# ReLU²-attention and a gated feed-forward: three blocks of k on ScalarE's queue instead of four, with k's first block cast first

## The chip, the cores and the metric

The kernel runs on one core of one Trainium2 chip. The metric is the device time of one execution in microseconds, the median of several. Times within an execution are counted from the start of the profiled span.

## The reference

The inputs are `q`, `k`, `v` of shape (8 batches, 12 heads, 448 positions, 64 dimensions) and the weights of a feed-forward layer, all f32.

```python
scores = scale * np.matmul(q, k.transpose(0, 1, 3, 2))   # scale = 1/sqrt(64)
attn = np.maximum(scores, 0.0) ** 2 / S                  # S = 448
attn_out = np.matmul(attn, v)
...
x = attn_out.transpose(0, 2, 1, 3).reshape(B * S, H * D) # (3584, 768)
h = x @ w_in                                             # (3584, 2048)
g = np.maximum(h, 0.0) + alpha * np.minimum(h, 0.0)
out = g @ w_out                                          # (3584, 768)
```

## The kernel before

The work is cut into 24 groups of four heads (a batch has three groups). The 448 positions of a head are held as 64 rows of 7 blocks, so a group's q or k is a tile of 128 partitions (two times 64 rows), 2 head pairs, 7 blocks and 64 dimensions. For each group q and k must be transposed so that the dimension lies on the partitions. For the first groups TensorE does it: `turn_pe` transposes some blocks with an identity matrix into a PSUM bank and copies them into a tile `T`, on VectorE ("D") or ScalarE ("A"), as each call says. Later groups use a DMA transpose.

Scores come one k block at a time: `sc` issues eight matmuls (`score_mm`, line 175) of one k block in `T` against all seven q blocks in `T`, into a pair of PSUM banks; a ReLU on ScalarE (line 184) or VectorE (line 186) brings them to SBUF as `rl`; `square` (line 194) squares them; `attnv` multiplies by v; `f1` and `f2` are the two feed-forward products. PSUM has eight banks, given out in turn by `take_pair` and `take_bank` to the one that was taken longest ago. TensorE is the busiest engine.

The order on each engine is written out by hand: the code runs under a manual schedule, and every engine executes its instructions in the order in which the code emits them. An instruction waits at the head of its engine's queue until what it reads is there.

The change is in the start, group 0. Its q and k come by three transfers. SyncE's queue loads all of q as f32 into `qfirst`; ScalarE's queue loads the first four blocks of k as f32 into `kfirst` (line 129); GpSimd's queue loads the other three blocks of k, cast to bf16 in flight, directly into `raw` (line 133). The f32 blocks are cast to bf16 by `cast0` (line 296) on ScalarE or VectorE, and then `turn_pe` (transposes on line 153, copies on line 156) builds `T`. While the data are under way, 36 matmuls of the identity (line 137) keep TensorE active.

Before, ScalarE's queue at the start is: casts of q blocks 4-5 and 6, casts of k blocks 0-1 and 2-3, copies into `T` of q 4-5, q 6, k 1, k 3, k 2, then the ReLU of score block 0. VectorE's is: casts of q 0-1 and 2-3, copies of q 0-1, q 2-3, k 0, the ReLU of score block 1, the copy of k 4-6, the squares of blocks 0 and 1. TensorE's is: transposes of q 0-1, q 4-5, q 2-3, q 6, k 0, k 1, k 3, k 2, scores 0, scores 1, transposes of k 4-6, scores 2, scores 3, transposes of group 1's q, scores 4 and 5, transposes of group 1's k.

Of the kernel before, what the change touches and what calls it, by code (L numbers as in the profile page):

```python
# [10 lines left out]
F32 = mybir.dt.float32  # L11
# [5 lines left out]
NJ = 7  # L17
# [3 lines left out]
def kernel(  # L21
# [10 lines left out]
    nc = tc.nc  # L32
    B, H, S, D = q.shape
# [11 lines left out]
    singles = ctx.enter_context(tc.tile_pool(name="singles", bufs=1))  # L45
# [40 lines left out]
    def take_bank():  # L86
        i = min(range(8), key=lambda i: (taken[i], i))
        take(i, 1)
        return psum[:, i]


    raw, vraw = {}, {}

    def load_qk(n, names="qk"):
        b, g = divmod(n, NG)
        for name in names:
            src = q if name == "q" else k
            t = raw_pool.tile([128, 2, NJ, D], BF16, tag=name, name=f"{name}raw")
            flat = src[b].rearrange("(m two) (pp j) d -> (two pp) m (j d)", two=2, j=NJ)
            nc.gpsimd.dma_start(out=t.rearrange("p m j d -> p m (j d)"), in_=flat[:, 2 * g:2 * g + 2])  # L100
            raw[(n, name)] = t

    def load_v(n):
        b, g = divmod(n, NG)
        t = v_pool.tile([128, 2, NJ, D], BF16, tag="v", name="vraw")
        flat = v[b].rearrange("(m two) (pp j) d -> (two pp) m (j d)", two=2, j=NJ)
        nc.gpsimd.dma_start(out=t.rearrange("p m j d -> p m (j d)"), in_=flat[:, 2 * g:2 * g + 2])  # L107
        vraw[n] = t
# [4 lines left out]
    def load_w_in(i):  # L113
        lo, hi = 512 * i, 512 * i + 512
        for hf in range(2):
            for e in range(2):
                nc.gpsimd.dma_start(out=w_in_sb[64 * hf:64 * hf + 64, :, e, lo:hi],  # L117
                                    in_=w_in_v[hf, e, :, :, lo:hi])
# [2 lines left out]
        for lo in range(lo, hi, step):  # L121
            nc.gpsimd.dma_start(out=w_out_sb[h][:, lo:lo + step], in_=w_out_v[:, lo:lo + step, COLS[h][0]:COLS[h][1]])

    FIRST = 4
    first, flat0 = {}, {}
    for name, src, eng, hi in (("q", q, nc.sync, NJ), ("k", k, nc.scalar, FIRST)):
        first[name] = singles.tile([128, 2, hi * D], F32, name=f"{name}first")
        flat0[name] = src[0].rearrange("(m two) (pp j) d -> (two pp) m (j d)", two=2, j=NJ)[:, :2]
        eng.dma_start(out=first[name], in_=flat0[name][:, :, :hi * D])
        raw[(0, name)] = raw_pool.tile([128, 2, NJ, D], BF16, tag=name, name=f"{name}raw")  # L130
    nc.sync.dma_start(out=alpha_sb, in_=moe_alpha.rearrange("(kf p) -> p kf", p=128))
    make_identity(nc, ident)
    nc.gpsimd.dma_start(out=raw[(0, "k")][:, :, FIRST:].rearrange("p m j d -> p m (j d)"),
                        in_=flat0["k"][:, :, FIRST * D:])
    warm = psum[:, 7, :128]
    for _ in range(36):
        nc.tensor.matmul(warm, ident, ident, start=True, stop=True)
    load_qk(1)
    load_v(0)
# [6 lines left out]
    def turn_pe(n, parts=(("q", 0, NJ, "D"), ("k", 0, NJ, "D"))):  # L146
        if n not in T:
            T[n] = T_pool.tile([128, 2, NJ, 128], BF16, tag="T", name="T")
        for name, lo, hi, eng in parts:
            ps = take_bank().bitcast(BF16)  # L150
            for j in range(lo, hi):
                for s in range(2):
                    nc.tensor.transpose(ps[64 * s:64 * s + 64, 128 * j:128 * j + 128], raw[(n, name)][:, s, j], ident)  # L153
            dst = T[n][:, "qk".index(name), lo:hi].rearrange("p j c -> p (j c)")
            copy = nc.vector.tensor_copy if eng == "D" else nc.scalar.copy
            copy(dst, ps[:, 128 * lo:128 * hi])  # L156
# [62 lines left out]
    def sc(chunks):  # L219

        for n, j, eng in chunks:
            late.append((n, j, relu(score_mm(n, j), eng)))
# [70 lines left out]

    def cast0(name, lo, hi, eng):
        copy = nc.vector.tensor_copy if eng == "D" else nc.scalar.copy
        copy(raw[(0, name)][:, :, lo:hi].rearrange("p m j d -> p m (j d)"), first[name][:, :, D * lo:D * hi])  # L296

    load_w_in(0)
    load_v(2)
    cast0("q", 4, 6, "A")  # L300
    cast0("q", 0, 2, "D")
    cast0("q", 6, 7, "A")
    cast0("q", 2, 4, "D")
    cast0("k", 0, 2, "A")
    cast0("k", 2, 4, "A")
    turn_pe(0, (("q", 0, 2, "D"),))
    turn_pe(0, (("q", 4, 6, "A"),))
    turn_pe(0, (("q", 2, 4, "D"),))
    turn_pe(0, (("q", 6, 7, "A"),))
    turn_pe(0, (("k", 0, 1, "D"),))  # L310
    turn_pe(0, (("k", 1, 2, "A"),))
    turn_pe(0, (("k", 3, 4, "A"),))
    turn_pe(0, (("k", 2, 3, "A"),))
    sc([(0, 0, "A")])
    sc([(0, 1, "D")])
    turn_pe(0, (("k", 4, 7, "D"),))
    load_qk(3)
    load_w_in(1)
    load_w_in(2)
# [243 lines left out]
```

## Time and profile before

| | before |
|---|---|
| time, median of 3 | 385.66 us (385.64 to 386.36) |
| profiled span | 383.8 us |
| PE busy | 374.8 us, 98% |
| VectorE busy | 266.3 us, 69% |
| ScalarE busy | 208.5 us, 54% |
| granted TensorE clock | 1.00 |

A timeline line gives the start, the time from the start of the first to the end of the last of a run of equal instructions, the engine, the line, the operation, the tile written and the tile read, and how many; in brackets, how long the engine sat idle before it and what ended that. PE is TensorE, ACT ScalarE, DVE VectorE, POOL GpSimd; `T<-psum` is a copy into `T`, `rl<-psum` a ReLU, `at<-rl` a square. The chain of waits is followed back from the last instruction of the program: each step goes to whatever released it. A DMA line ends with the size and the time from issue to landing.

### The profile page before, as it was taken

What the parts mean: (1) busy time and instruction counts of PE and PEld (TensorE: products, weight loads), DVE (VectorE), ACT (ScalarE), POOL (GpSimd) and SP (SyncE); (2) the same over time, 40 slices, a digit from 0 to 9 for tenths busy, and PEclk for the clock granted to TensorE, in tenths of its full rate; (3) what the DMA queues carried; (4) which work ended last, traced back from release to release, by engine and by line L of the source; (5) the groups of instructions that cost most, each with busy time, mean ns of one, the idle gap of its engine ahead of it and who ended that gap; (6) DMA issues with size and microseconds to landing.
All of it is one profiled execution on the core that took longest, in us unless ns stands there. A gap on an engine that the chain in (4) does not pass through costs nothing.

```text
span 383.8 us, 7855 instructions
## 1 busy us (share of the span) xinstructions
PE 374.8 (98%) x3179; PEld 206.0 (54%) x3200; DVE 266.3 (69%) x422; ACT 208.5 (54%) x339; POOL 68.3 (18%) x104
## 2 busy tenths in 40 slices
PE   7799999999999999999999999999999999999996
PEld 5454565555544455555565455544556445645554
DVE  3997988767757988688656887779855788526300
ACT  6988687445643754555444556546544465434321
POOL 8566050506302202022200222020000000000000
PEclk9999999999999999999999999999999999999999
DMA  9999989999998658597292772946045300120023
GB/s 160 186 204 202 184 138 209 168 196 114 233 203 134 106 110 120 106 127 120 55 165 61 128 122 50 167 86 110 15 89 84 77 0 16 43 68 2 14 70 83
DMA packets 73284, 43.42 MB, mean 113 GB/s; under 512 B 40352, under 2 KB 69792, under 8 KB 73248
## 3 DMA queue, kind: packets, MB, share of 16 engines
q0 software_dynamic: 26864, 22.45, 40.2%
q1 hardware_dynamic: 45952, 20.07, 27.2%
q8 instruction: 25, 0.41, 0.4%
q10 hardware_dynamic: 432, 0.39, 0.3%
q14 instruction: 11, 0.09, 0.1%
HBM read 45.62 MB, written 11.01 MB: 148 GB/s over the span
## 4 chain that ended last, share of the span: by engine, by line
PE 94%; DVE 2%; DMA 1%; ACT 1%; issue 0%; ACTq 0%; DVEq 0%
PE psum L238 38%; PE psum L263 38%; PE psum L175 9%; PE psum L204 8%; DMA qfirst<-in_q_dram 1%; DVE at L194 1%; DVE T L156 1%; DVE rl L186 0%; PE psum L153 0%; ACT osb L265 0%; ACT kraw L296 0%; ACT qraw L296 0%; ACTq L271 0%; ACT T L156 0%; DVEq L186 0%
## 5 line engine op out<-in xcount | busy, mean ns | idle before, releaser
L263 PE MATMUL psum<-w_out,gT 128*128 128x256 bf16 (+3 forms) x891 | 149.8, 322 | 1.1
L238 PE MATMUL psum<-xT,w_in_sb 128*128 128x448 bf16 x768 | 149.8, 353 | 0.0
L263 PEld LDWEIGHTS <-gT 128*128 128x128 bf16 x912 | 86.8, 98 | 64.2 <-issue 8.2
L238 PEld LDWEIGHTS <-w_in_sb 128*128 128x128 bf16 x768 | 73.6, 98 | 72.8 <-issue 6.0
L247 DVE SCALAR_TENSOR_TENSOR gT<-neg,beta_sb,psum 128x448 bf16<-128x448 f32 x128 | 83.5, 677 | 33.7 <-ACT neg L246 33.5
L246 ACT ACTIVATE neg<-psum 128x448 f32<-128x448 f32 x128 | 69.3, 547 | 60.3 <-PE psum L238 58.5
L184 ACT ACTIVATE rl<-psum 128x896 bf16<-128x896 f32 x112 | 97.7, 929 | 1.0 <-PE psum L175 1.0
L194 DVE TENSOR_TENSOR at<-rl 128x896 bf16<-128x896 bf16 x162 | 90.6, 618 | 0.0
L186 DVE TENSOR_SCALAR rl<-psum 128x896 bf16<-128x896 f32 x56 | 60.8, 1086 | 39.9 <-PE psum L175 39.8
L265 ACT COPY osb<-psum 128x256 f32<-128x256 f32 (+3 forms) x57 | 27.0, 473 | 104.7 <-PE psum L263 98.9
L175 PE MATMUL psum<-T 64*64 64x448 bf16 x672 | 45.4, 356 | 2.1 <-ACT rl L184 1.0
L100 POOL DMA_DIRECT2D qraw<-in_q_dram x23 | 16.6, 722 | 133.6 <-DVE perm L161 130.3
L204 PE MATMUL psum<-at,vraw 64*64 64x448 bf16 x672 | 36.2, 350 | 0.0
L175 PEld LDWEIGHTS <-T 64*64 64x64 bf16 x672 | 16.9, 105 | 20.9 <-issue 13.6
L204 PEld LDWEIGHTS <-vraw 64*64 64x64 bf16 x672 | 21.0, 106 | 11.7 <-issue 1.5
L215 DVE TENSOR_SCALAR xT<-psum 128x448 bf16<-128x448 f32 x24 | 15.0, 624 | 14.6 <-PE psum L204 10.8
L100 POOL DMA_DIRECT2D kraw<-in_k_dram x23 | 16.7, 727 | 7.8 <-DVE rl L186 5.2
L107 POOL DMA_DIRECT2D vraw<-in_v_dram x24 | 17.5, 731 | 2.9 <-DMA qraw<-in_q_dram 1.1
L214 ACT ACTIVATE xT<-psum 128x448 bf16<-128x448 f32 x24 | 13.4, 560 | 2.3 <-PE psum L204 2.3
L161 DVE COPY perm<-kraw 128x896 bf16<-128x896 bf16 x19 | 11.6, 609 | 0.8 <-DMA kraw<-in_k_dram 0.8
L161 DVE COPY perm<-qraw 128x896 bf16<-128x896 bf16 x19 | 11.6, 612 | 0.0
L117 POOL DMA_DIRECT2D w_in_sb<-in_moe_w_in_dram x16 | 10.1, 634 | 6.6 <-DMA w_in_sb<-in_moe_w_in_dram 2.9
(25 smaller groups left out, 43.0 us busy)
## 6 DMA issues: line engine op xcount, KB each, us to landing
out_dram<-osb SPq DMA_DIRECT2D x54, 128.0 KB, 2.4
vraw<-in_v_dram POOLq DMA_DIRECT2D x24, 224.0 KB, 8.1
qraw<-in_q_dram POOLq DMA_DIRECT2D x23, 224.0 KB, 5.3
kraw<-in_k_dram POOLq DMA_DIRECT2D x23, 224.0 KB, 6.6
out_dram<-osb SPq DMA_DIRECT2D x56, 64.0 KB, 2.2
w_in_sb<-in_moe_w_in_dram POOLq DMA_DIRECT2D x16, 192.0 KB, 8.1
w_out<-in_moe_w_out_dram POOLq DMA_DIRECT2D x4, 512.0 KB, 8.8
w_out<-in_moe_w_out_dram POOLq DMA_DIRECT2D x4, 256.0 KB, 8.7
```

The lines of the kernel that those rows point to most:

```text
L100: nc.gpsimd.dma_start(out=t.rearrange("p m j d -> p m (j d)"), in_=flat[:, 2 * g:2 * g + 2])
L161: nc.vector.tensor_copy(p[:, i], raw.pop((n, name)).rearrange("p s j d -> p j s d"))
L175: nc.tensor.matmul(ps[64 * c:64 * c + 64, r, :S], t[64 * r:64 * r + 64, 1, j, 64 * c:64 * c + 64], t[64 * r:64 * r + 64, 0, :, 64 * c:64 * ...
L184: nc.scalar.activation(rl, ps[:, :, :S], ACTF.Relu)
L186: nc.vector.tensor_scalar(rl, ps[:, :, :S], 0.0, None, ALU.max)
L194: nc.vector.tensor_tensor(a, rl, rl, ALU.mult)
L204: nc.tensor.matmul(ps[64 * s:64 * s + 64, r, :S], vv[64 * r:64 * r + 64, s, j, :], a[64 * r:64 * r + 64, s], start=(j == 0), stop=(j == NJ ...
L238: nc.tensor.matmul(ps, w_in_sb[:, km // 2, km % 2, bass.ts(ff, 128)], xT[b][:, km // 2, km % 2, :], start=(km == 0), stop=(km == KM - 1))
L246: nc.scalar.activation(neg, ps, ACTF.Relu, scale=-1.0)
L247: nc.vector.scalar_tensor_tensor(gT[b // 2][:, ff, (b % 2) * S:(b % 2) * S + S], neg, beta_sb[:, ff:ff + 1], ps, ALU.mult, ALU.add)
L263: nc.tensor.matmul(ps, gT[sb][:, ff, bass.ts(c, 128)], w_out_sb[h][:, ff, lo:hi], start=(ff == 0), stop=(ff == KF - 1))
L265: nc.scalar.copy(o[:, lo:hi], ps)
```

## The change

Three things change, all in group 0. ScalarE's queue loads k's blocks 0 to 2 instead of 0 to 3, and GpSimd's queue the other four. ScalarE casts k's block 0 alone, ahead of its casts of q, and k's blocks 1-2 only after its copies of q into `T`. The copies of k's blocks into `T` are divided anew: block 1 goes to VectorE by itself, block 2 stays on ScalarE, and block 3 is transposed and copied with the tail 4-6, by VectorE. There are two warm-up matmuls fewer. It is meant to have less f32 data of k to wait for and to cast before the first scores, and to give ScalarE fewer copies.

In the changed kernel ScalarE's queue is: cast k 0, casts q 4-5 and q 6, copies q 4-5 and q 6, cast k 1-2, copy k 2, then the ReLU of block 0. VectorE's is: casts q 0-1 and 2-3, copies q 0-1, q 2-3, k 0, k 1, the ReLU of block 1, the copy of k 3-6, the squares. TensorE's is: transposes q 0-1, q 4-5, q 2-3, q 6, k 0, k 1, k 2, scores 0, scores 1, transposes k 3-6, scores 2, scores 3, and on as before.

```diff
-    FIRST = 4
+    FIRST = 3
...
-    for name, src, eng, hi in (("q", q, nc.sync, NJ), ("k", k, nc.scalar, FIRST)):
-        first[name] = singles.tile([128, 2, hi * D], F32, name=f"{name}first")
+    for name, lo, hi, eng in (("q", 0, NJ, nc.sync), ("k", 0, FIRST, nc.scalar)):
+        t = singles.tile([128, 2, (hi - lo) * D], F32, name=f"{name}first{lo}")
+        eng.dma_start(out=t, in_=flat0[name][:, :, lo * D:hi * D])
...
-    for _ in range(36):
+    for _ in range(34):
...
+    cast0("k", 0, 1, "A")
+    cast0("q", 0, 2, "D")
     cast0("q", 4, 6, "A")
-    cast0("q", 0, 2, "D")
+    cast0("q", 2, 4, "D")
     cast0("q", 6, 7, "A")
-    cast0("q", 2, 4, "D")
-    cast0("k", 0, 2, "A")
-    cast0("k", 2, 4, "A")
     turn_pe(0, (("q", 0, 2, "D"),))
     turn_pe(0, (("q", 4, 6, "A"),))
     turn_pe(0, (("q", 2, 4, "D"),))
     turn_pe(0, (("q", 6, 7, "A"),))
     turn_pe(0, (("k", 0, 1, "D"),))
-    turn_pe(0, (("k", 1, 2, "A"),))
-    turn_pe(0, (("k", 3, 4, "A"),))
+    cast0("k", 1, 3, "A")
+    turn_pe(0, (("k", 1, 2, "D"),))
     turn_pe(0, (("k", 2, 3, "A"),))
     sc([(0, 0, "A")])
     sc([(0, 1, "D")])
-    turn_pe(0, (("k", 4, 7, "D"),))
+    turn_pe(0, (("k", 3, 7, "D"),))
```

More of the change, by code (lines that the diff above doesn't have):

```diff
@@ L122, in load_w_out @@
             nc.gpsimd.dma_start(out=w_out_sb[h][:, lo:lo + step], in_=w_out_v[:, lo:lo + step, COLS[h][0]:COLS[h][1]])
-    FIRST = 4
+    FIRST = 3
     first, flat0 = {}, {}
-    for name, src, eng, hi in (("q", q, nc.sync, NJ), ("k", k, nc.scalar, FIRST)):
-        first[name] = singles.tile([128, 2, hi * D], F32, name=f"{name}first")
+    for name, src in (("q", q), ("k", k)):
         flat0[name] = src[0].rearrange("(m two) (pp j) d -> (two pp) m (j d)", two=2, j=NJ)[:, :2]
-        eng.dma_start(out=first[name], in_=flat0[name][:, :, :hi * D])
         raw[(0, name)] = raw_pool.tile([128, 2, NJ, D], BF16, tag=name, name=f"{name}raw")
+    for name, lo, hi, eng in (("q", 0, NJ, nc.sync), ("k", 0, FIRST, nc.scalar)):
+        t = singles.tile([128, 2, (hi - lo) * D], F32, name=f"{name}first{lo}")
+        eng.dma_start(out=t, in_=flat0[name][:, :, lo * D:hi * D])
+        for j in range(lo, hi):
+            first[(name, j)] = t[:, :, (j - lo) * D:]
     nc.sync.dma_start(out=alpha_sb, in_=moe_alpha.rearrange("(kf p) -> p kf", p=128))
@@ L295, in cast0 @@
         copy = nc.vector.tensor_copy if eng == "D" else nc.scalar.copy
-        copy(raw[(0, name)][:, :, lo:hi].rearrange("p m j d -> p m (j d)"), first[name][:, :, D * lo:D * hi])
+        copy(raw[(0, name)][:, :, lo:hi].rearrange("p m j d -> p m (j d)"), first[(name, lo)][:, :, :D * (hi - lo)])
     load_w_in(0)
     load_v(2)
+    cast0("k", 0, 1, "A")
+    cast0("q", 0, 2, "D")
     cast0("q", 4, 6, "A")
-    cast0("q", 0, 2, "D")
+    cast0("q", 2, 4, "D")
     cast0("q", 6, 7, "A")
-    cast0("q", 2, 4, "D")
-    cast0("k", 0, 2, "A")
-    cast0("k", 2, 4, "A")
     turn_pe(0, (("q", 0, 2, "D"),))
```

## The prediction

> **What bounds the kernel now.** I read the page's part 4 first, then the chain of waits in order of time over the first 20 us, then the timelines of ScalarE (ACT), VectorE (DVE) and TensorE (PE), and the DMA view of the first 7 us.
>
> ```profile
> PE 94%; DVE 2%; DMA 1%; ACT 1%; issue 0%; ACTq 0%; DVEq 0%
> ```
>
> The chain is TensorE for 94% of the span. The rest is the start:
>
> ```profile
> 0.74 4.21 DMA qfirst<-in_q_dram
> ...
> 4.97 0.60 ACT qraw L296 x2
> 5.57 0.61 ACT kraw L296 x2
> 6.18 0.44 ACT T L156 x2
> ...
> 6.67 0.60 PE psum L175 x8
> ...
> 7.37 1.09 DVE rl L186
> 8.46 0.26 DVE T L156
> 8.72 1.07 DVE at L194 x2
> 9.79 1.06 DVE T L156 x2
> ...
> 16.05 0.57 PE psum L175 x8
> 16.62 1.34 PE psum L204 x28
> ```
>
> (Columns: start, length, what, all in us.) q lands at 4.95, ScalarE casts and copies until the first scores at 6.67; from 7.37 to 16.05 VectorE carries the chain without a hole worth naming; from 16.05 on it is TensorE. So a delay of VectorE's queue before 16 us goes one for one into the end, and that is where the change works.
>
> ```profile
> 4.97 0.60 ACT L296 CAST qraw<-qfirst 128x256 bf16<-128x256 f32 x2 [2.41 <-DMA qfirst<-in_q_dram]
> 5.48 0.70 ACT L296 CAST kraw<-kfirst 128x256 bf16<-128x256 f32 x2
> 6.09 1.03 ACT L156 COPY T<-psum 128x256 bf16<-128x256 bf16 x5
> 7.10 8.21 ACT L184 ACTIVATE rl<-psum 128x896 bf16<-128x896 f32 x10
> ```
>
> ScalarE: no gap from 4.97 to 15.3. Ten ReLUs in 8.21 us, so one starts every 0.80.
>
> ```profile
> 8.07 0.38 PE L175 MATMUL psum<-T 64*64 64x448 bf16 x4 [0.22 <-ACT rl L184]
> ```
>
> These are the scores of block 3. They wait for a PSUM pair only, freed by ScalarE's first ReLU (7.10 + 0.92 = 8.02). Their operand was ready since 7.12.
>
> ```profile
> qfirst<-in_q_dram SPq DMA_DIRECT2D x1, 448.0 KB, 4.2
> kfirst<-in_k_dram ACTq DMA_DIRECT2D x1, 256.0 KB, 4.6
> ```
>
> Both are issued at 0.74: q lands at 4.95, k at 5.34. k is the later one, and it still costs nothing before, because ScalarE casts q until 5.57 anyway.
>
> [...] instructions appear in the order that the code emits. A waiting head therefore holds everything behind it; my forecast rests on this. [...] 256 KB of k, issued together with 448 KB of q, land 0.4 us after it. [...] The warm-up shows it: its matmuls start every 0.107 us until 4.43 and every 0.056 after 4.6.
>
> **The change part by part.**
>
> *Transfers.* k on ScalarE's queue goes from 256 to 192 KB. In the DMA view of 0 to 7 us the slices around 4 us move 370 to 430 GB/s; at 400 the 64 KB are worth 0.16 us. So k lands at about 5.34 - 0.16 = 5.2 (bounds: 5.1, if the 261 GB/s of the stretch 2 to 4 us counts, and 5.37 for no gain), and q, sharing with it, at about 4.84. The rest of k grows by as much; it landed at 1.43 + 5.3 = 6.7 and would now land about 6.9, while its transposes come at 7.9 below: hidden. Two warm-up matmuls fewer end at 4.8 instead of 5.05; TensorE then waits for q anyway: nothing.
>
> *Work moved.* ScalarE loses one cast in size (two of 128x256, 0.40 each, become one of 128x128, 0.29, and one of 128x256) and two T copies of 128x128: one goes to VectorE alone (k's block 1), one joins VectorE's copy of k's tail, 512 columns in place of 384 (0.35 for 384 and 0.62 for 896, so 0.42). By issue spacing (cast 0.31 and 0.20, copy 0.16) ScalarE saves 0.11 + 0.32 = 0.43 us. It would gain that if it were only busy and never waiting.
>
> *Waits added.* There are three, and I walk the queues with the durations of before (an instruction on ScalarE starts some 0.09 before its predecessor's end; from an engine's end to a dependant's start 0.04 to 0.05; a transpose 0.22; four score matmuls 0.38; a PE switch between scores and transposes 0.15 to 0.3, as at 6.90 to 7.17 and 7.31 to 7.46).
>
> First wait: ScalarE's first cast is now k's block 0, which needs the later transfer. It runs 5.22 to 5.51. Behind it q 4-5 ends at 5.82 (was 5.38) and q 6 at 6.02 (was 5.57). TensorE, in order, stands at q 4-5: transposes of q 4-5, q 2-3, q 6 and k 0 start at 5.88, 6.01, 6.12, 6.18. All T copies of q and k 0 are done by 6.78 (ScalarE's q 6 at 6.75, VectorE's k 0 at 6.78).
>
> Second wait: k's blocks 1-2 are cast on ScalarE behind its two copies of q, 6.64 to 7.04. Their transposes are emitted before the first scores, so TensorE holds scores 0, whose operands are ready at 6.8, until they are through: transposes at 7.09 and 7.17, scores 0 at 7.33 (was 6.67). ScalarE's copy of block 2 ends at 7.73 and its first ReLU starts at 7.76 (was 7.10, +0.66). VectorE's copy of block 1 runs 7.38 to 7.61, scores 1 go 7.66 to 8.04, and VectorE's ReLU of block 1 starts at 8.17 (was 7.37, +0.80; the 0.13 from scores to this ReLU are those of before).
>
> Third wait: block 3's T copy is now part of VectorE's tail copy, behind that ReLU (1.09 long, next start 1.01 later): 9.18 to 9.59. Scores 3 start at 9.65 instead of 8.07. Queued behind them on TensorE are group 1's q transposes (8.38 before, now 9.95), scores 4 and 5, and group 1's k transposes (9.40 before; spacing from scores 3 of 1.33 is kept, so 10.98). ScalarE's ReLU of block 2 starts at 8.72 and ends at 9.63; its ReLU of block 3 can start only at 10.08 (was 8.71, +1.37), an idle stretch of some 0.45. VectorE, after squares 0 and 1 and group 1's q copy, which ends near 11.2, waits for the last k transpose at 11.56 and copies at 11.60; before it did so at 10.24.
>
> *Sum.* VectorE's copy of group 1's k is late by 11.60 - 10.24 = 1.36; ScalarE's ReLUs are late by 1.37 to 1.40. From there on both queues hold the same work as before without slack (both busy 2.00 of every 2 us in the window sums from 10 to 18), so group 2's T copies, and TensorE's scores at 16.05, come 1.4 later, and so does the end: 385.66 + 1.4 = 387.06. The 0.43 us taken off ScalarE are spent inside its waits.
>
> **The rivals.**
>
> *k lands with or ahead of q* (the smaller transfer overtakes). Then wait one vanishes: q's casts start at about 4.86, scores 0 near 6.76, VectorE's ReLU near 7.6; but scores 3 still wait for the tail copy, to 9.09, and group 1's k copy comes at about 11.03: +0.8, 386.45. Against it: equal numbers of packets, and k last in the trace.
>
> *Faster.* If scores 0 were limited by ScalarE's amount of work, as the chain's 1.65 us of ScalarE pieces (4.97 to 6.62) suggest, taking off 0.43, and 0.11 for q's earlier landing, would give 385.12. Against it: transposes of k 1-2 stand ahead of the scores in the queue, and two of the three waits are not work of ScalarE.
>
> *Absorbed.* Some of the delay falls into holes: TensorE is busy only 1.3 to 1.6 of every 2 us between 9 and 17 us. About half lost, 386.2. Against it: VectorE and ScalarE, which set those holes, have none themselves.
>
> *Clock lost.* [...] The scores and transposes of about 2 us of TensorE work then take up to twice as long, half of it exposed: 1 us more, 388.1. Against it: the pauses are under 1 us each, and before had some of 0.6 without harm.
>
> **How the numbers follow.** The walk 58%, k early 14%, absorbed 10%, faster 10%, clock 8%. The likeliest gives 387.06. With k's landing between 5.1 and 5.37 the walk spans +1.26 to +1.55; k early and absorbed reach down to 386.2, and 0.2 to 0.3 for my switching times goes below that: 386.0. The high end, 387.7, has the same margin above the walk. Outside lie the faster and the clock case, under 2 in 10. 0.2% is 0.77 us. Over it lie the walk, the clock and half of k early (which sits on the line): 0.73. Within it lie the other half of k early, the absorbed case and half of the faster one: 0.22. The rest, 0.05, is a faster case that also closes some of TensorE's holes between 9 and 17 us.
>
> **What would show it.** Right: kfirst lands near 5.2, ScalarE's first cast starts at that landing and not at q's; the first scores start near 7.3, behind k 1-2's transposes; scores 3 wait for a VectorE T copy and start near 9.65; ScalarE has a hole ahead of its third ReLU; the scores at 16.05 move to about 17.4, and from there to the end nothing differs. Wrong: kfirst landing before 5.0, first scores before 6.7, or the delay at the 16 us scores not reaching the end.

## The result, and the profile after

| | before | after |
|---|---|---|
| time, median of 4 | 385.67 us (385.64 to 386.36) | 388.82 us (388.40 to 389.07) |
| profiled span | 383.8 us | 387.3 us |

The changed kernel is slower by 3.15 us, a ratio of 1.0076 (95% interval 1.0059 to 1.0094). The direction was forecast; the size, 1.4 us, was less than half of it.

The chain of waits of the changed kernel, in order of time (start, length, what, in us):

```profile
0.74 4.88 DMA kfirst<-in_k_dram
...
5.64 0.30 ACT kraw L299
...
7.35 0.31 ACT kraw L299
...
7.71 0.42 PE psum L156 x4
8.13 0.92 PE psum L178 x7
...
9.15 1.09 DVE rl L189
10.25 0.34 DVE T L159
...
19.74 0.57 PE psum L178 x8
```

The chain begins with k's transfer, no longer q's, and goes to and fro between ScalarE and TensorE: this is the queue that the prediction walked. But group 2's scores come at 19.74 instead of 16.05, 3.7 us late, not 1.4. From there to the end nothing is added; the span is 3.5 us longer.

ScalarE's timeline shows the holes in brackets:

```profile
5.64 0.30 ACT L299 CAST kraw<-kfirst 128x128 bf16<-128x128 f32 x1 [3.09 <-DMA kfirst<-in_k_dram]
...
8.70 0.92 ACT L187 ACTIVATE rl<-psum 128x896 bf16<-128x896 f32 x1 [0.27 <-PE psum L178]
10.16 0.92 ACT L187 ACTIVATE rl<-psum 128x896 bf16<-128x896 f32 x1 [0.54 <-PE psum L178]
11.27 0.92 ACT L187 ACTIVATE rl<-psum 128x896 bf16<-128x896 f32 x1 [0.19 <-PE psum L178]
```

Before, ScalarE had none between 4.97 and 15.3. And TensorE's timeline, in three stretches:

```profile
1.36 3.81 PE L140 MATMUL psum<-ident 128*128 128x128 bf16 x34 [1.36 <-POOL ident masks.py:199]
...
8.06 0.96 PE L178 MATMUL psum<-T 64*64 64x448 bf16 x8
...
10.63 0.59 PE L178 MATMUL psum<-T 64*64 64x448 bf16 x4 [0.52 <-DVE T L159]
...
18.51 0.57 PE L178 MATMUL psum<-T 64*64 64x448 bf16 x8
```

The eight score matmuls at 8.06 take 0.96 us; the same eight take 0.57 at 18.51, and took 0.57 before at 6.67. A single score matmul takes 0.58 us until 16.2 and 0.35 to 0.37 from 18.5. The 34 warm-ups start every 0.107 us to the last. So TensorE's clock was at half until 16.8, where the trace records its first change, and not only until 4.55, as in the kernel before. Nothing in the queues explains that.

This profile is of the slowest of the four executions. The other three carry a mean granted clock of 0.991: 0.009 of 386.6 us is 3.5 us, which is what 7 us at half clock lose. So by this estimate they lost the clock too, after a first release.

One theory was left, and three rivals. *Walk*: the three waits cost 1.4 us, or 1.8 with k landing at 5.62 instead of 5.2, and the half clock comes on top as an effect of its own. The rivals: the clock explains it all; the two warm-ups fewer are what lost the clock; or the moment of release is drawn anew at each execution, and the times scatter.

### The profile page after: what moved, and what is told of

Same layout as the page of the kernel before. It is cut to its first block, busy times and chain, and to the rows that moved or that the text cites. A ratio compares the mean times of both kernels' runs of the same rounds, so it can differ in the third digit from the quotient of the medians.

```text
span 387.3 us, 7872 instructions
## 1 busy us (share of the span) xinstructions
PE 379.1 (98%) x3198; PEld 207.4 (54%) x3198; DVE 266.5 (69%) x423; ACT 209.0 (54%) x337; POOL 68.2 (18%) x104
## 4 chain that ended last, share of the span: by engine, by line
PE 95%; DVE 2%; DMA 1%; ACT 1%; issue 0%; ACTq 0%; DVEq 0%
PE psum L241 38%; PE psum L266 38%; PE psum L178 9%; PE psum L207 8%; DMA kfirst<-in_k_dram 1%; PE psum L156 1%; DVE at L197 1%; DVE T L159 0%; DVE rl L189 0%; ACT osb L268 0%; ACT kraw L299 0%; ACT T L159 0%; ACTq L274 0%; ACT qraw L299 0%; DVEq L189 0%
## 5 line engine op out<-in xcount | busy, mean ns | idle before, releaser
L178 PE MATMUL psum<-T 64*64 64x448 bf16 x672 | 47.1, 371 | 1.4 <-DVE T L159 1.4
```

What stands on the lines that cost most here:

```text
L178: nc.tensor.matmul(ps[64 * c:64 * c + 64, r, :S], t[64 * r:64 * r + 64, 1, j, 64 * c:64 * c + 64], t[64 * r:64 * r + 64, 0, :, 64 * c:64 * ...
```

## The experiments

Each is timed against runs of the kernel before on the same chip, and "over before" is the difference of the two medians.

### Is it the number of warm-ups?

`a36` and `a40` are the changed kernel with 36 and 40 warm-ups, `b34` is the kernel before with 34.

```diff
-    for _ in range(34):
+    for _ in range(36):
```

> The changed kernel with 36 warm-up matmuls instead of 34, nothing else. In the changed kernel's trace TensorE's matmuls run at half clock until 17.0 us (warm-ups every 0.107 us to the last one, 128x448 score matmuls 0.58 us), in the kernel before only until 4.5 us. Theory count (the two warm-ups fewer keep the clock from being released): clock released near 4.5 us again, time 387.1 +- 0.3. Theory pauses (TensorE's longer waits after 4.9 us do it): as the changed kernel, 388.4 to 389.1. Theory phase ([...] the release time is drawn at each execution): the runs scatter between 387 and 389 whatever the count.

> The changed kernel with 40 warm-up matmuls, which reach to about 5.6 us at half clock and so up to the first transposes. Theory count: 387.1 +- 0.3, clock released by 5 us. Theory pauses: between 387.3 and 388.8, since the first pause (4.97 to 5.50) is filled and the two later ones are not. Theory phase: scatter between 387 and 389.

> The kernel before with 34 warm-up matmuls instead of 36, nothing else. Theory count: the clock is released late here too, and the time rises by 1 to 2.5 us, to 386.7 to 388.2. Theory pauses: 385.7, as before, since the warm-ups end before q lands in either case. Theory phase: scatter.

Measured: `a36` 388.46 (2.84 over before), `a40` 388.44 (2.82; one of four executions at 387.04), `b34` 385.57 (0.05 under before). The two warm-ups were not it: given back they recover about 0.3 us at most (the intervals of `a36`, 1.0054 to 1.0084, and of the changed kernel overlap), and taken from the kernel before they cost nothing. Nor do the times scatter freely: of the twelve executions of the changed kernel, `a36` and `a40`, eleven lie between 388.29 and 389.12.

The windows view suggests why. The trace of `a36` records the clock from 6.04 us on: full for 3.41 us, then half for 10.24, three times as long, then full. Here it is divided at these changes and every 3.41 us (stretch, its length, then the busy time of PE, PEld, DVE, ACT and POOL, granted clock, DMA share, GB/s; PEld is TensorE's loading of weights). In the first row the clock reads 1.00 only because the record has not begun; the warm-ups in it start every 0.107 us, at half clock:

```profile
2.63:6.04 3.41, 3.12 (x32) 2.69 (x30) 0.86 (x3) 0.67 (x3) 3.41 (x6) 1.00 1.23 210
6.04:9.46 3.42, 2.12 (x36) 1.08 (x36) 1.78 (x6) 2.69 (x7) 2.47 (x5) 1.00 1.22 186
9.46:12.87 3.41, 3.03 (x40) 1.76 (x40) 2.02 (x4) 2.29 (x4) 2.01 (x3) 0.50 1.26 203
12.87:16.28 3.41, 2.99 (x32) 1.17 (x27) 3.15 (x6) 3.35 (x5) 1.57 (x3) 0.50 1.18 168
16.28:19.70 3.42, 3.31 (x45) 2.24 (x48) 3.42 (x7) 3.03 (x5) 2.20 (x4) 0.50 1.23 196
19.70:23.11 3.41, 3.38 (x72) 2.38 (x65) 3.20 (x7) 3.41 (x6) 1.89 (x4) 1.00 1.25 204
```

Read the PE column against the clock of the next row. The warm-ups and first transposes fill 3.12 of 3.41 us, 91%, and the clock is full in the next window. In that one TensorE, kept waiting, is busy 2.12 us, 62%, and the clock falls to half. After 89% and 88% it stays at half; after 97% it is full, from 19.7 on. Here is the kernel before, divided the same way:

```profile
1.14:4.55 3.41, 3.19 (x31) 3.19 (x32) 0.00 (x0) 1.28 (x1) 3.28 (x6) 1.00 0.73 211
...
11.38:14.79 3.41, 2.32 (x44) 1.36 (x43) 3.41 (x7) 3.41 (x5) 1.54 (x3) 1.00 1.15 168
```

The window of the warm-ups has 94%, and the emptiest of the start after it 68%: in this profile the clock never falls there. The changed kernel's own profile begins with windows of 79%, 84% and 85% at half clock, and only after the fourth, 94%, is the clock full, from 16.78 on:

```profile
3.13:6.54 3.41, 2.70 (x30) 2.20 (x29) 0.79 (x3) 0.80 (x3) 3.41 (x6) 1.00 1.33 218
...
13.37:16.78 3.41, 3.21 (x34) 1.32 (x31) 2.86 (x6) 3.36 (x5) 1.97 (x3) 1.00 1.15 155
```

### Do fillers in the waits give the clock back?

`afill` puts 14 identity matmuls into TensorE's two longer early waits. `ahold` adds 40 warm-ups, 10 matmuls ahead of scores 3, and issues the score matmuls of five blocks twice (same bank, same result). `bhold` is the control, the kernel before with these five blocks doubled. In the excerpt below the first two additions are in both `afill` and `ahold`; the third is `ahold`'s alone, and the last is in `ahold` and `bhold`.

```diff
+    fill(6)
     turn_pe(0, (("q", 4, 6, "A"),))
...
     cast0("k", 1, 3, "A")
+    fill(8)
     turn_pe(0, (("k", 1, 2, "D"),))
...
+    fill(10, 6)
     sc([(0, 3, "A")])
...
+        for rep in range(2 if (n, j) in AGAIN else 1):
```

> The changed kernel with 34 warm-ups and 14 more matmuls of the identity in TensorE's two later waits: six ahead of the transposes of q's blocks 4-5, eight ahead of those of k's blocks 1-2. They write the bank of the warm-ups, which is free then. Theory count: as the changed kernel, 388.4 to 389.1, clock released late. Theory pauses: clock released by about 8 us instead of 17, time 387.1 to 387.9. Theory phase: scatter.

> The changed kernel with TensorE kept busy: 40 warm-ups, 6 and 8 identity matmuls in its two early waits, 10 ahead of scores 3, and the score matmuls of blocks (0,6) and (1,0) to (1,3) issued twice into the same bank with the same result. If the changed kernel's loss is the queue walk (1.4 us, with k landing at 5.4 instead of 5.2: 1.5) plus the half clock (the rest of 3.15), the clock now stays up from about 5 us on and the time is 387.1 +- 0.3. If the walk is wrong and the clock explains it all, 385.7 to 386.2. If filling cannot hold the clock, as with the 14 fillers, 387.6.

> The kernel before with the score matmuls of blocks (0,6) and (1,0) to (1,3) issued twice, as the control: what the doubled matmuls themselves cost. The kernel before falls in a part of its executions to 386.2 to 386.4 with a granted clock of 0.996. If that is a lost clock window in the sparse stretch from 11 to 15 us, these executions vanish and all lie at 385.5 to 385.7. If the doubled matmuls are on the path: slower, up to 386.4.

Measured: `afill` 387.61 (1.99 over before), `ahold` 387.38 (1.72; ratio 1.0044, interval 1.0029 to 1.0059), `bhold` 385.61 (0.05 under; 0.9996, 0.9987 to 1.0004). More work for TensorE took 1.43 us off the changed kernel's 3.15. In `afill`'s profile the clock still fell once, behind its sparse stretch:

```profile
11.84:15.25 3.41, 2.04 (x26) 0.76 (x25) 3.36 (x7) 3.41 (x6) 1.78 (x3) 1.00 1.21 176
15.25:18.66 3.41, 3.26 (x44) 2.26 (x44) 3.41 (x7) 3.01 (x6) 2.15 (x4) 0.50 1.20 187
```

60% busy at full clock, then half. That one window may have cost little: two of `afill`'s four executions carry a mean clock of 1.00 and are at most 0.12 us faster (though 1.00 can hide a late first release), and `afill` and `ahold` can't be told apart by their times (`afill`'s ratio is 1.0044 too). In `ahold`'s profile the clock is full from 4.64 us on. What remains is seen in its chain:

```profile
5.55 0.30 ACT kraw L301
...
17.78 0.57 PE psum L180 x8
```

Group 2's scores are 1.73 us late, with every matmul after the warm-ups at full speed. The doubled matmuls cost the kernel before nothing, and the executions at 386.2 to 386.5 that `b34` and the kernel before have are gone in `bhold` (12 executions, all at or below 385.89). They too look like a lost window: their mean clock is 0.996, which is about 3 us at half, and none of the 44 executions of `bhold`, `b_w1` and `b_w3`, all with the doubled blocks, carries it. No profile shows one.

### Does the clock alone cost time, without a changed queue?

`b20` is the kernel before with 20 warm-ups instead of 36 (the edit is the count).

> The kernel before with 20 warm-up matmuls instead of 36: no queue and no wait is changed, and the warm-ups end at 3.5 us, before q lands. If the clock follows the share of busy time in windows of 3.41 us (0.92 or more needed to release it, as the profiles so far show), it is released late or not before 10 us, and the time rises by 1 to 2.5 us with nothing else changed. If the clock loss comes only with the changed kernel's waits: 385.5 to 386.4 as before.

Measured: 386.44, 0.86 over before (1.0018, 1.0011 to 1.0025), a little under the low end expected. Its windows:

```profile
3.23:6.64 3.41, 1.78 (x27) 1.32 (x24) 1.24 (x5) 1.70 (x7) 3.41 (x6) 1.00 1.30 212
6.64:10.06 3.42, 3.42 (x42) 1.78 (x44) 2.27 (x5) 2.77 (x6) 2.42 (x4) 1.00 1.24 192
```

No release after 52%; matmuls at half speed then fill the next window entirely, and the clock is full from 10.06 on. So here a late release cost 0.86 us without any wait of the changed kernel. In the changed kernel's profile the half clock lasts longer, to 16.78, through windows of 79%, 84% and 85% to the one of 94%.

### What is each wait worth, with the clock held?

`ahold_no1` and `no1` cast k's block 0 behind ScalarE's casts of q (wait one out); `ahold_no2` casts k's blocks 1-2 ahead of ScalarE's copies (wait two out); `no12` does both. `no1` and `no12` have 36 warm-ups, the doubled blocks and no fillers ahead of q 4-5, and `no12` none ahead of k 1-2 either. The edit of `no12`'s queue, against the changed kernel:

```diff
-    cast0("k", 0, 1, "A")
     cast0("q", 0, 2, "D")
     cast0("q", 4, 6, "A")
     cast0("q", 2, 4, "D")
     cast0("q", 6, 7, "A")
+    cast0("k", 0, 1, "A")
+    cast0("k", 1, 3, "A")
...
-    cast0("k", 1, 3, "A")
     turn_pe(0, (("k", 1, 2, "D"),))
```

> The filled changed kernel with k's block 0 cast behind ScalarE's two casts of q instead of ahead of them (wait one of the walk taken out, the others kept). Walk: q's casts start at q's landing again, scores 0 come 0.5 earlier, and so the time falls by 0.4 to 0.6 against the filled changed kernel, to about 386.6. If wait one is hidden by the two behind it: no difference (within 0.15).

> The filled changed kernel with k's blocks 1-2 cast directly behind ScalarE's casts of q, ahead of its copies of q (wait two of the walk taken out, the others kept). Walk: scores 0 then wait for ScalarE's copy of q 6 only, about 0.4 to 0.5 earlier, so the time falls by 0.3 to 0.5 against the filled changed kernel. If the scores' start does not set the end: no difference (within 0.15).

> Wait one again, since in the last such run the 40 warm-ups and the six fillers behind them ran at half clock to 6.1 us and stood on the path themselves. Now 36 warm-ups, no fillers ahead of q's blocks 4-5, the other fillers kept; k's block 0 cast behind ScalarE's casts of q. Walk: scores 0 at 7.0 to 7.2 instead of 7.68, time 0.4 to 0.6 under the filled changed kernel's 387.2 to 387.4, so 386.8 +- 0.2. If wait one is hidden by the others: 387.2 to 387.5.

> Waits one and two out: ScalarE casts q 4-5, q 6, k 0 and k 1-2 and only then copies; 36 warm-ups, fillers only ahead of scores 3. What is left of the change is wait three (block 3 in VectorE's tail copy) and block 1's copy on VectorE. Walk: scores 0 near 6.8, scores 3 near 8.9 (before 8.07), time 386.1 to 386.4. If wait three costs nothing: 385.6 to 385.8.

`ahold_no1` (387.70) does not answer the question. In its profile the 40 warm-ups ran at half clock, and they and the six fillers behind them stood on the path: first scores at 8.27. `ahold_no2` (387.18, against 387.38 for `ahold`) gained 0.2, less than expected and less than its executions spread; there the eight fillers stand on the path in place of the wait. Without such fillers, `no1` is at 386.57 (1.08 over before) and `no12` at 385.89 (0.40 over), both a little faster than expected. So wait one is worth 1.72 - 1.08 = 0.64 us, wait two 1.08 - 0.40 = 0.68, and 0.40 are left for wait three, less what little `no12` gains ahead of it. The split is rough: `ahold` has four executions from 387.17 to 387.93, and in the slower ones its fillers may stand on the path as in `ahold_no1`. In the profiles group 2's scores are 1.73 us late in `ahold`, 0.96 in `no1` (17.01) and 0.41 in `no12` (16.46), which gives 0.77, 0.55 and 0.41. `no12`'s chain:

```profile
4.90 0.60 ACT qraw L301 x2
...
6.52 0.60 PE psum L180 x8
...
7.22 1.09 DVE rl L191
8.31 0.34 DVE T L159
...
8.70 0.38 PE psum L180 x4
```

It starts from q again, and the first scores come at 6.52, 0.15 before the 6.67 of the kernel before. Of that 0.07 is q's earlier landing; the rest, 0.08, is ScalarE's saved work. Then VectorE's ReLU and its tail copy stand ahead of scores 3, at 8.70 instead of 8.07.

### Waits three and one by themselves

`ahold_no3` and `no123` take wait three out by giving block 3 a transpose and a ScalarE copy of its own. `b_w3` goes the other way and puts it, alone, into the kernel before; `b_w1` puts wait one there (both with the doubled blocks of `bhold`). `no123` is `no12` with this edit and without the ten fillers ahead of scores 3, which `ahold_no3` leaves out too.

```diff
# ahold_no3, no123
-    turn_pe(0, (("k", 3, 7, "D"),))
+    turn_pe(0, (("k", 3, 4, "A"),))
+    turn_pe(0, (("k", 4, 7, "D"),))
# b_w3
-    turn_pe(0, (("k", 3, 4, "A"),))
...
-    turn_pe(0, (("k", 4, 7, "D"),))
+    turn_pe(0, (("k", 3, 7, "D"),))
# b_w1
+    cast0("k", 0, 2, "A")
     cast0("q", 4, 6, "A")
...
-    cast0("k", 0, 2, "A")
```

> The filled changed kernel with wait three alone out: block 3 transposed behind scores 1 and copied by ScalarE behind its first ReLU, VectorE's tail copy 384 columns again. Walk: scores 3 at about 9.4 instead of 10.0, time 0.4 to 0.6 under the filled changed kernel's 387.2 to 387.4, so 386.8 +- 0.2. If scores 3 are not what holds group 1's transposes: no difference.

> All three waits out: as the last one, and block 3 transposed by itself behind scores 1 and copied by ScalarE behind its first ReLU, so that scores 3 don't wait for VectorE; 36 warm-ups, no fillers but the doubled score matmuls, which cost the kernel before nothing. k still loads three blocks on ScalarE's queue. Walk: what remains is 0.1 to 0.3 us of ScalarE's order, time 385.6 to 386.0. If the smaller transfer of k itself costs something: above 386.2.

> Wait three alone, put into the kernel before (with the doubled score matmuls, which cost it nothing): block 3 of k is transposed and copied with blocks 4-6 by VectorE behind its first ReLU, and nothing else is changed. Walk, with the 0.43 us that the kernel with waits one and two taken out still lay behind: scores 3 at 8.8 to 8.9 instead of 8.07, time 386.0 to 386.3. If a score block that waits for VectorE instead of ScalarE costs nothing: 385.5 to 385.7.

> Wait one alone, put into the kernel before (with the doubled score matmuls): ScalarE casts k's blocks 0-1 ahead of its casts of q, so that q waits for k's landing. k still comes as four blocks. Walk: everything of ScalarE behind the first cast is late by k's landing minus q's (5.37 - 4.95) plus nothing, so 0.4 us, time 386.0 +- 0.2. If k's landing is not what holds ScalarE: 385.5 to 385.7.

`no123` (386.07, 0.58 over before) and `ahold_no3` (387.16, 1.67 over) missed their expectations: taking wait three out gave nothing. One more group of transposes takes one more PSUM bank, and the code gives out the bank that was taken longest ago. The tail's transposes then take a bank of the pair that scores 2 had. Scores 2 go onto the pair of scores 0, behind ScalarE's ReLU, and scores 3 onto the pair of scores 1, behind VectorE's. `ahold_no3`'s timeline of TensorE:

```profile
9.84 0.38 PE L180 MATMUL psum<-T 64*64 64x448 bf16 x4 [0.34 <-ACT rl L189]
10.44 0.38 PE L180 MATMUL psum<-T 64*64 64x448 bf16 x4 [0.21 <-DVE rl L191]
```

Scores 2 (the first line) now wait for a ReLU, which they did not before, and so do scores 3. A new wait took the old one's place. (In this profile, as in `ahold_no1`'s, warm-ups and fillers at half clock also stand on the path; in `no123`'s there are no fillers.)

`b_w3` shows wait three from the other side: 386.14, 0.56 over before (1.0007, 1.0000 to 1.0014, at the edge of what can be told), and its profile is plain. TensorE's timeline there:

```profile
8.88 0.38 PE L177 MATMUL psum<-T 64*64 64x448 bf16 x4 [0.95 <-DVE T L156]
```

Scores 3 wait 0.95 us for VectorE's copy and start at 8.88, as expected (8.8 to 8.9). `b_w1` is at 385.97, 0.39 over before (0.9999 to 1.0016 as a ratio, so at the edge too), the 0.4 that the two landings differ by; its ScalarE starts at 5.35 with k instead of 4.97 with q.

## Why the prediction was wrong

**Direction and path: right.** The chain moved as forecast. ScalarE's first cast waits for k, TensorE holds the first scores behind k 1-2's transposes, and scores 3 wait for VectorE's tail copy. The order within a queue held in the trace: q has landed by 5.16, when VectorE casts its part of it; ScalarE casts its own part only at 5.85, behind the cast of k that waited until 5.64. With the clock held (`ahold`), ScalarE's hole ahead of its third ReLU is 0.43 us, against 0.45 forecast.

**The walk's sum: right, but for one term.** At held clock the three waits measure 1.72 us (the interval is 1.1 to 2.3) against 1.4 forecast. Taken out one after another they are 0.64, 0.68 and 0.40, which add up to 1.72 by construction; put alone into the kernel before, wait one is 0.39 (k there lands 0.4 after q) and wait three 0.56, which is evidence of its own. Wait two was not put in alone. The term that was mis-sized is the landing of k. I took off 0.16 us for 64 KB less, to 5.2. In the ten profiles with three blocks k took 4.5 to 4.8 us from its issue, and 4.9 in the changed kernel's first; in the six with four blocks 4.6 to 4.7. The smaller transfer lands no sooner. In `ahold`'s profile (4.8, cast at 5.55 instead of 5.22) that is the missing 0.33: its first scores start at 7.68, against 7.33 in my walk, and group 2's scores are 1.73 late, against 1.4. With the usual landing, 4.6, the miss is about half of that. Why 64 KB don't matter was not tried; k's queue has 272 packets in either kernel, only shorter ones after the change.

**The step that failed: "Clock lost", 8%.** I set it aside because "the pauses are under 1 us each, and before had some of 0.6 without harm". That looks at each pause by itself. What the profiles show beside a lost clock is how much TensorE did in a whole 3.41 us window: `a36`, `afill` and `a40` (6.74 to 10.15, busy 1.90 of 3.41 us) lost it after 62%, 60% and 56%, and the kernel before, which kept it, had 68% in its emptiest. I had sized the effect at 1 us, from some 2 us of TensorE work at half speed (in `a36` the half clock lasted 10.24 us), and put it in the wrong place, as a rival instead of a term: the waits that I had just summed are TensorE's idle time, so the more of them I found, the emptier its windows became. With fillers to hold its clock the changed kernel loses 1.72 us instead of 3.15. The other 1.43 is the clock's part by subtraction; that the 1.72 is the waits' is borne out by the walk, which gives 1.73 once k's landing in `ahold`'s profile is put in.

**The claim that two warm-ups fewer cost nothing: right** in the kernel before (`b34`); in the changed kernel they cost 0.3 us at most (`a36`).

**The rivals "k early", "faster" and "absorbed": wrong.** No profile shows k ahead of q; ScalarE's saved work is real but small (0.08 us at the first scores of `no12`) and spent by wait three; and of the delay at group 2's scores no more than about 0.2 us is absorbed by the end (3.7 us there, 3.5 in the span).

## What to carry to other kernels

When an edit puts a wait ahead of TensorE, cost it twice: once along the queue (1.72 us here), and once as matmul work in each stretch of 3.41 us, since windows with too little of it were paid for again at half clock (1.43 us here), which lasted 10.24 us in `a36` and 3.41 in `afill`. In this start a window that was 62% busy was followed by half clock (`a36`) and one of 63% was not (the changed kernel, 16.78 to 20.19); the next section shows why the percentage itself does not carry over. Put a cast ahead of another only if its data land first (in `b_w1` they land 0.4 us later, and that cost 0.39); emit what the first scores don't need behind them (wait two, 0.68 us); and when a copy is moved or split, look at which PSUM bank everything after it gets (in `ahold_no3` two score blocks then waited 0.34 and 0.21 us for ReLUs). Fillers tested for a lost clock cheaply (`afill` took 1.16 us off), but only where the engine waits anyway: in `ahold_no1` they stood on the path, and the first scores came at 8.27 instead of 7.68.

## What the runs showed of the hardware

- The changes of the clock that the traces record are whole steps of 3.41 us apart: 3.41 and 10.24 us in `a36`, and in the kernel before 378.88 us (4.55 to 383.43, 111 steps).
- Full clock, at the start: windows of 56% (`a40`), 60% (`afill`) and 62% (`a36`) busy were each followed by half clock. Windows of 63% (the changed kernel, 16.78 to 20.19), 68% (the kernel before, 11.38 to 14.79) and 72% (`afill`, 8.43 to 11.84) were not.
- Half clock: after windows of 91% (`a36`), 94% (the kernel before and the changed one), 96% (`ahold`), 97% (`a36`) and 100% (`a40`, `b20`) the clock was full. After 52% (`b20`), 79%, 84% and 85% (the changed kernel), 88% and 89% (`a36`) it stayed at half.
- The percentage alone does not sort the windows. This one, at the end of the changed kernel, is 51% busy, with matmuls that use the whole 128*128 array, and the clock is still full from there to the end of the span (385.41 to 387.30 reads 1.00). In the kernel before the last window, 3% busy (380.02 to 383.43), was followed by 0.50. What is counted instead was not shown.

```profile
382.00:385.41 3.41, 1.74 (x22) 1.27 (x19) 0.00 (x0) 0.74 (x2) 0.00 (x0) 1.00 0.36 96
```

- The first release came at 4.55 us in the kernel before and at 6.04 in `a36`, with 36 warm-ups in each; at 4.64 in `ahold` and 6.74 in `a40`, with 40 in each; at 10.06 in `b20` with 20, and at 16.78 in the changed kernel with 34.
- The granted clock reads 1.00 before its first recorded change, even where matmuls run at half speed: the changed kernel's profile says 1.00 throughout. The spacing of the warm-ups, 0.107 us at half clock and 0.056 at full, shows it.
